# Attention in front of a routed MLP: the u term beside the logits, the state's decay on VectorE, bounds by transposes, another prologue

## The chip, the core and the metric

One core of a Trainium2 chip runs the whole program. The metric is the device time of one execution in microseconds (us), median of three runs. TensorE (PE), VectorE (DVE), ScalarE (ACT), GpSimd (POOL) and the DMA queue of SyncE (SP) each work through their instructions in the order written and wait for each other by semaphores.

## The reference, cut to what matters

```python
for t in range(S):                                   # 4 batches, 8 heads, 768 steps, head size 48
    cur = einsum('bhd,bhe->bhde', u[None] * kt, vt)
    y[:, :, t] = einsum('bhd,bhde->bhe', rt, state + cur)
    state = w[None, :, :, None] * state + einsum('bhd,bhe->bhde', kt, vt)
...
logits = x @ w_gate                                  # x: y by token, 3072 x 384; 8 experts
order = np.argsort(-logits.flatten())                # greedy, 384 tokens to an expert
h = np.maximum(x[mask] @ w1[e], 0.0); out[mask] = h @ w2[e]
...
h = np.maximum(x @ w_in, 0.0); return h * h @ w_out  # a second MLP over all tokens
```

## The kernel before

Attention works in 24 chunks n of 128 tokens, chunk c = n // 4 of batch b = n % 4. Per chunk `prep` (L175, DVE) multiplies r and k by powers of w, `prep_rk` (L179, POOL) makes pr = r*k, `qk` (L209, PE) makes the 128x128 scores of 8 heads in two PSUM banks pA0, pA1, and `am` (L212, DVE) copies their lower triangle over AM, which `diagonal` (L198, POOL) has filled with the u term of each head on its diagonal. That term, cc, is the sum over d of u*r*k: `ruk` (L189, PE) makes it with pr as weights, `ccput` (L193, DVE) copies it out. `state_y` (L221) adds r*T of the state T to pY, `chunk_y` (L228) adds AM*v, and `yev` (L234, ACT) copies pY to YT. `kvm` makes the next state in PSUM: Wd*T (L283), the decay by a diagonal matrix, and kk*v (L287), kk = k*KT from `prep_kk` (L203, POOL); `tput` (L293, ACT) copies it to T. One iteration later YT gives the router's logits (`logits` L242, `lev` L246, `logits_by_token` L249, `lput` L254) and x by token (`by_token` L260, `xput` L269 on ACT, then a DMA to DRAM, xd).

The loop over n writes these out by hand in one order for all engines: at its top what waits for the iteration before (lput, xput, ccput), then work for chunks ahead (prep_rk n+3, diagonal n+2, prep_kk and qk n+1, prep n+4, am n+1), then state_y to tput of chunk n, and at its end by_token n-1, ruk n+3 and logits_by_token n-1. Loads run up to 6 (rk) and 4 (tk) chunks ahead on SP.

Between these, `R.step` issues single DVE instructions of the routing from a list that `pace` fills at n-1 = 8, 16 and 20. `spread` takes the largest and smallest router key of the first 16 chunks over all partitions with `G.partition_all_reduce` (L456, POOL); `grid0` lays 64 thresholds between them (L507 to L510), `count` compares (L520) and counts on PE. After the loop `close0` does the rest; `between` there puts the last chunks' x to DRAM. Then `phase` searches the first expert's threshold in steps of compares (L447, DVE) and counts (L612, PE), the tokens are gathered from xd (L717), and the two MLPs follow, expert by expert, bound by PE.

Of the kernel before, what the change touches and what calls it, by code (L numbers as in the profile page):

```python
# [25 lines left out]
FT = mybir.dt.float32  # L26
# [10 lines left out]
NC = S // C  # L37
# [16 lines left out]
def attention(ctx, tc, a, R, L, xd):  # L54
# [12 lines left out]
    AHEAD_RK, AHEAD_TK = 6, 4  # L67

# [17 lines left out]
    Uw = att.tile([112, 4, 8], FT, name="Uw")  # L86
# [4 lines left out]
    wg = att.tile([128, 2, 2, 64], FT, name="wg")  # L91
# [9 lines left out]
    YT = [att.tile([128, 2, 2, 128], FT, name=f"yt{j}") for j in range(2)]  # L101
    KT = att.tile([128, 400], FT, name="KT")
    V.memset(Pw[:, :, :, 0:1], 1.0)
# [38 lines left out]
    for eng, W, x in ((V, WR, 0), (G, WK, 1)):  # L142
        eng.tensor_tensor(W.rearrange("p i (a b) -> p i a b", a=16),
                          Qw[:112, x, :, :, None].to_broadcast([112, 4, 16, 8]),
                          Pw[:112, x, :, None, :].to_broadcast([112, 4, 16, 8]), op=OP.mult)
    W128 = att.tile([112, 4, 1], FT, name="W128")
    TT = att.tile([112, 4, 128], FT, name="TT")
    Wd = att.tile([112, 2, 4, 64], FT, name="Wd")

    def decays():  # L150
        V.tensor_tensor(Uw, Uw, sq[:112, 0, :, 0:1].to_broadcast([112, 4, 8]), op=OP.mult)
        V.tensor_tensor(W128, sq[:112, 0, :, 6:7], sq[:112, 0, :, 6:7], op=OP.mult)
        G.tensor_tensor(TT, WK, W128.to_broadcast([112, 4, 128]), op=OP.mult)
# [9 lines left out]
    def decay_diagonals():  # L163
        sh = [112, 4, 64]
        for s in range(2):
            G.tensor_tensor(Wd[:, s], ident[:112, None, half(s, 64)].to_broadcast(sh), W128.to_broadcast(sh), op=OP.mult)


    pr, cc, kks, pA, AM, pYs, pk, pts, pls, lts, pms = ({} for _ in range(11))
# [11 lines left out]
    def pm(n):  # L181
        if n not in pms:
            pms[n] = ps.tile([128, 136], FT, name="pm")
        return pms[n]

    def ruk(n, m):

        for i in range(4):
            PE.matmul(pm(m)[:, 128:], pr[n][:, i], Uw[:, i], start=not i, stop=i == 3)  # L189

    def ccput(n, m):
        cc[n] = wk.tile([128, 8], FT, name="cc")
        V.tensor_copy(cc[n], pm(m)[:, 128:])  # L193

    def diagonal(n):

        AM[n] = wk.tile([128, 4, 2, 128], FT, name="AM", bufs=3)
        G.affine_select(AM[n].rearrange("p i s t -> p (i s) t"), cc[n][:, :, None].to_broadcast([128, 8, 128]),  # L198
                        pattern=[[0, 8], [1, 128]], compare_op=OP.is_equal, fill=0.0, base=0, channel_multiplier=-1)
# [31 lines left out]
    def yev(n, s, eng=None):  # L231
        o, x = YT[n % 2][:, s], pYs[n][s]
# [5 lines left out]
    def logits(n):  # L238
# [9 lines left out]
    def logits_by_token(n, m):  # L248
        PE.transpose(pm(m)[:, :128], lts[n], ident)  # L249

    def lput(n, m):
        c, b = divmod(n, B)
        x = pm(m)[:, :128].rearrange("p (s e) -> p e s", s=2)[:, :8]
        V.tensor_reduce(L[:, b * NC + c, :], x, axis=AX.X, op=OP.add)  # L254

    def by_token(n):
        pts[n] = ps.tile([128, 4, 128], FT, name="pt")
        for s in range(2):
            for j in range(2):
                PE.transpose(pts[n][:, 2 * s + j], YT[n % 2][:, s, j], ident)  # L260

# [12 lines left out]
    def kvm(n):  # L274

        c, b = divmod(n, B)
        if c == NC - 1:
            return
        p = pk[n] = ps.tile([128, 4, 64], FT, name="pk")
        if c:  # L280
            for i in range(4):
                for s in range(2):
                    PE.matmul(p[half(s, 64), i], Wd[:, s, i], T[b][:, i], start=not i, stop=False, skip_group_check=True)  # L283
        for i in range(4):
            for s in range(2):
                h = 2 * i + s
                PE.matmul(p[half(s, 64), i], kks[n][:, 48 * h:48 * h + 64], v_of(n, h), start=not c and not i, stop=True,  # L287
                          skip_group_check=True)
# [7 lines left out]
    ok = lambda n: 0 <= n < NCH  # L296
    decays()
    prep(0)
    prep_rk(0)
    decays_by_token()  # L300
    qk(0)
    ruk(0, -3)
    ccput(0, -3)
    diagonal(0)
    prep(1)
    prep_rk(1)
    ruk(1, -2)
    ccput(1, -2)
    prep_kk(0)
    diagonal(1)  # L310
    am(0, 0)
    am(0, 1)
    prep(2)
    prep_rk(2)
    ruk(2, -1)
    decay_diagonals()
# [4 lines left out]
    for n in range(NCH):  # L321
        load_rk(n + AHEAD_RK)
        load_tk(n + AHEAD_TK)
        if n == NCH - B:
            R.cnt0 = ps.tile([128, 512], FT, name="pk")
        if ok(n - 2):
            lput(n - 2, n - 1)
            xput(n - 2)
        if ok(n + 2):
            ccput(n + 2, n - 1)  # L330
        if ok(n + 3):
            prep_rk(n + 3)
        if ok(n + 2):
# [22 lines left out]
        kvm(n)  # L356
        tput(n)
# [6 lines left out]
        if ok(n - 1):  # L364
            logits_by_token(n - 1, n)
        R.step(4)
    n = NCH - 1
    lput(n - 1, n)
    logits(n)
    lev(n)  # L370
    logits_by_token(n, n + 1)
    lput(n, n + 1)
    R.arrive(NC - 1, NC)

    def last():
        xput(n - 1)
        by_token(n)
        xput(n)
# [4 lines left out]
class Routing:  # L383
# [4 lines left out]
    def __init__(self, tc, pool, ident, L):  # L388
        self.tc, self.pool, self.ident, self.L = tc, pool, ident, L
        self.misc = None  # L390
        self.todo, self.wide, self.mms, self.left = [], [], [], 0
        self.fill = lambda n=1: None
        self.lag = 3, 1
# [4 lines left out]
    def make(self):  # L398
# [13 lines left out]
        self.ones = one([128, 128], "onesb", BF)  # L412
        V.memset(self.ones, 1.0)
# [35 lines left out]
    def spread(self, gm):  # L449

        V, G = self.tc.nc.vector, self.tc.nc.gpsimd
        mx = self.tile([128, 2], "mx")
        junk = self.tile([128, NT], "sel")
        return [lambda: V.tensor_reduce(mx[:, 0:1], self.key0, axis=AX.X, op=OP.max),
                lambda: V.tensor_scalar(junk, self.low0, -1.0, -BIG, op0=OP.mult, op1=OP.max, accum_out=mx[:, 1:2]),
                lambda: G.partition_all_reduce(gm, mx, channels=128, reduce_op=bass.bass_isa.ReduceOp.max)]  # L456
# [27 lines left out]
    def arrive(self, c0, c1):  # L484

        V = self.tc.nc.vector
        l, m, cx, oh, lw = (self.chunks(t, c0, c1) for t in (self.L, self.key0, self.cx0, self.oh0, self.low0))
        self.todo.append(lambda: V.tensor_reduce(m, l, axis=AX.X, op=OP.max))
        ops = self.pick(l, m, cx, oh, self.tile([128, B, c1 - c0, E], "eq", FT, 1))
        least = lambda: V.tensor_reduce(lw, l, axis=AX.X, op=OP.min)  # L490
        if c1 < NC:
            self.todo += ops + [least]
        else:

            self.count(c0, c1)
            self.gm1 = self.tile([128, 2], "gm")
            mx0, mx1, red = self.spread(self.gm1)
            self.todo += [ops[0], least, ops[1], mx0, ops[2], mx1, red, ops[3]]

    def grid0(self):  # L500
# [3 lines left out]
        *mx, red = self.spread(gm)  # L504
        pause = lambda: None
        self.todo += mx + [pause, red, pause, pause, pause,
# [584 lines left out]
def _layouts(r, k, v, w, u, w_gate, w1, w2, w_in, w_out):  # L1091
# [13 lines left out]
    ul = np.zeros((112, 4, E), u.dtype)  # L1105
    for h in range(H):
        ul[64 * (h % 2):64 * (h % 2) + D, h // 2, h] = u[h]
    wg = np.zeros((128, 2, 2, 64), w_gate.dtype)
    for h in range(H):
# [8 lines left out]
        "wg": wg.reshape(128, 256),  # L1118
# [25 lines left out]
```

## Time and profile before

| | us |
|---|---|
| median of 3 runs (890.19 to 895.34) | 890.65 |
| profiled execution, device time | 890.34 |
| its span, first to last instruction | 888.3 |
| attention, first instruction to the first gather | 184.26 |

The profiled execution is one of the program's executions; 2.0 us of it lie around the span. In the rows below a time is us from the start of the span, then the length in us, the engine and line of the program, output<-inputs, the shape, and how many instructions the row merges; PEld is the load of TensorE's weights. "[x <-y]" is idle time of that engine just before, and what ended it. An fp32 matmul shows as two records.

### The profile page before, as it was taken

The page shows a single profiled execution, that of the slowest core. Times are in us where ns is not written, and L with a number is a line of the kernel's source. Part 1 is how long each engine was busy: PE and PEld are TensorE (multiplying, and loading weights), DVE is VectorE, ACT ScalarE, POOL GpSimd, SP SyncE. Part 2 cuts the span into 40 slices and gives each one's busy share as a digit, 9 for nine tenths or more (in the row PEclk, how much of TensorE's full clock was granted, in tenths as well). Part 3 has the DMA queues.
Part 4 walks back from the last instruction along what each step waited for, and adds up shares of the span by engine and source line. Part 5 has one row for each costly group of instructions (what it writes and reads, how often), then busy time and mean ns, then how long its engine had stood idle before and what let it go on. Part 6 is the DMA issues. An engine that isn't in the chain of part 4 may idle for free.

```text
span 888.3 us, 16748 instructions
## 1 busy us (share of the span) xinstructions
PE 813.9 (92%) x6497; PEld 775.3 (87%) x6497; DVE 439.5 (49%) x1016; ACT 366.1 (41%) x799; POOL 337.7 (38%) x322
## 2 busy tenths in 40 slices
PE   3899996668788699999999999999999999999997
PEld 2899995548678699999999989999999999999996
DVE  3645443669999735714651573259235512321211
ACT  0233331233354533642464265417533644554443
POOL 5877762138486640504143141405040506204001
PEclk9999997768799899999999999999999999999999
DMA  8775640145535210401231031105010404101000
GB/s 233 214 222 181 189 139 20 38 133 166 173 107 178 62 46 25 129 1 45 60 93 45 1 114 39 45 1 151 2 45 23 130 10 136 52 1 45 1 1 28
DMA packets 37503, 73.78 MB, mean 83 GB/s; under 512 B 5680, under 2 KB 25264, under 8 KB 37424
## 3 DMA queue, kind: packets, MB, share of 16 engines
q1 hardware_dynamic: 34352, 63.28, 23.9%
q0 software_dynamic: 3072, 9.44, 3.3%
q8 instruction: 51, 0.84, 0.4%
q14 instruction: 28, 0.23, 0.1%
HBM read 63.26 MB, written 9.44 MB: 82 GB/s over the span
## 4 chain that ended last, share of the span: by engine, by line
PE 78%; DVE 15%; issue 2%; POOL 1%; DMA 1%; ACT 1%; POOLq 0%; SPq 0%; DVEq 0%; ACTq 0%
PE acc L784 10%; PE acc L785 10%; PE acc L786 10%; PE ph L784 10%; PE ph L786 9%; PE ph L785 9%; PE pA L209 3%; PE pm L189 3%; PE pY L228 2%; PE misc L612 2%; DVE cm L447 2%; DVE raw L835 2%; DVE raw L831 2%; DVE al L962 2%; PE pl L242 2%
## 5 line engine op out<-in xcount | busy, mean ns | idle before, releaser
L781 POOL TENSOR_TENSOR wl<-raw,wh 128x384 fp32r<-128x384 f32 x120 | 125.9, 1067 | 159.6 <-ACT wh L780 131.0
L962 DVE TENSOR_TENSOR al<-t,ah 128x384 fp32r<-128x384 f32 x120 | 86.4, 723 | 158.9 <-ACT t L959 155.6
L784 PE MATMUL ph<-YH,wi 128*128 128x384 f32 x384 | 132.6, 345 | 0.0
L784 PE MATMUL acc<-wo,ah 128*128 128x384 f32 x384 | 131.2, 342 | 0.0
L786 PE MATMUL acc<-wo,al 128*128 128x384 f32 x384 | 130.2, 339 | 0.6 <-POOL al L962 0.6
L785 PE MATMUL acc<-wo,ah 128*128 128x384 f32 x384 | 129.6, 338 | 0.0
L785 PE MATMUL ph<-YL,wi 128*128 128x384 f32 x384 | 129.0, 336 | 0.0
L786 PE MATMUL ph<-YH,wi 128*128 128x384 f32 x384 | 128.9, 336 | 0.0
L977 POOL DMA_INDIRECT out_dram<-rows,idx x24 | 23.7, 989 | 253.3 <-ACT rows L975 249.1
L955 ACT ACTIVATE t<-ph 128x384 f32<-128x384 f32 x128 | 62.5, 488 | 138.0 <-PE ph L786 136.9
L780 ACT ACTIVATE wh<-raw 128x384 fp32r<-128x384 f32 x128 | 65.1, 523 | 65.4 <-PE ph L785 20.8
L925 DVE SCALAR_TENSOR_TENSOR al<-ph,ah 128x384 fp32r<-128x384 f32 x64 | 35.2, 551 | 85.0 <-ACT ah L924 79.2
L786 PEld LDWEIGHTS acc<-wo,al 128*128 128x128 f32 x384 | 73.0, 190 | 1.2 <-POOL al L962 1.2
L785 PEld LDWEIGHTS acc<-wo,ah 128*128 128x128 f32 x384 | 73.0, 190 | 0.0
L784 PEld LDWEIGHTS acc<-wo,ah 128*128 128x128 f32 x384 | 72.9, 190 | 0.1
L784 PEld LDWEIGHTS ph<-YH,wi 128*128 128x128 f32 x384 | 72.6, 189 | 0.3
L785 PEld LDWEIGHTS ph<-YL,wi 128*128 128x128 f32 x384 | 72.7, 189 | 0.0
L786 PEld LDWEIGHTS ph<-YH,wi 128*128 128x128 f32 x384 | 72.5, 189 | 0.0
L785 PE MATMUL acc<-al,wh 128*128 128x384 f32 x192 | 66.1, 344 | 4.0 <-DVE al L925 4.0
L784 PE MATMUL acc<-ah,wh 128*128 128x384 f32 x192 | 68.2, 355 | 1.5 <-ACT ah L924 1.5
L447 DVE TENSOR_TENSOR cm<-key,thr 128x512 bf16<-128x512 f32 (+2 forms) x81 | 68.4, 879 | 0.3
L959 ACT ACTIVATE t<-t 128x384 f32<-128x384 f32 x128 | 67.1, 524 | 2.8
(205 smaller groups left out, 1576.6 us busy)
## 6 DMA issues: line engine op xcount, KB each, us to landing
raw<-in_w_dram SPq DMA_DIRECT2D x128, 192.0 KB, 2.5
rk<-in_rk_dram SPq DMA_DIRECT2D x24, 448.0 KB, 4.5
tk<-in_tk_dram SPq DMA_DIRECT2D x24, 392.0 KB, 8.6
raw<-in_wi_dram SPq DMA_DIRECT2D x16, 384.0 KB, 5.5
raw<-in_wo_dram SPq DMA_DIRECT2D x16, 384.0 KB, 3.0
xd<-xs SPq DMA_DIRECT2D x24, 192.0 KB, 1.8
rows<-xd,idx POOLq DMA_INDIRECT x24
out_dram<-rows,idx POOLq DMA_INDIRECT x24
```

The lines of the kernel that those rows point to most:

```text
L189: PE.matmul(pm(m)[:, 128:], pr[n][:, i], Uw[:, i], start=not i, stop=i == 3)
L209: PE.matmul(pA[n][s][:, i], RK[n][half(s), 1, i], RK[n][half(s), 0, i], start=True, stop=True)
L447: eng.tensor_tensor(cm, key[:, :, None].to_broadcast(sh), th, op=OP.is_ge)
L780: A_.activation(hi, t, AF.Copy)
L781: (eng or G).tensor_tensor(lo, t, hi.bitcast(FT), op=OP.subtract)
L784: PE.matmul(o, l[0], r[0], start=first, stop=False)
L785: PE.matmul(o, l[0], r[1], start=False, stop=False)
L786: PE.matmul(o, l[1], r[0], start=False, stop=last)
L925: later(1, lambda: V.scalar_tensor_tensor(hl, o, 0.0, hh.bitcast(FT), op0=OP.max, op1=OP.subtract))
L955: A_.activation(t, o, AF.Relu)
L959: A_.activation(t, t, AF.Square)
L962: later(2, lambda: (G if p == 0 and f < 8 else V).tensor_tensor(gl, t, gh.bitcast(FT), op=OP.subtract))
```

## The change

(`LATE` is 6; `R.spare` gives the bank of `by_token`.)

- u term: `ruk` and its weights pr leave the loop. `logits` now writes four quarters of 32 partitions of its bank: two with the logits' weights, 32 columns wide, and two with Uw (32 columns wide) as weights and pr[n+3] moving. `lev` and `logits_by_token` carry both; `ccput(n + 2)` reads the u term from the bank that `lput(n - 2)` reads. The first four chunks still use `ruk`.
- diagonals: POOL fills half of AM, ACT the other half by four scaled copies of the identity.
- decay: the diagonal matrices Wd and their 8 matmuls leave `kvm`. `fade` makes tT = T*W128 on DVE, `tput` adds it to kk*v on DVE.
- bounds: `partition_all_reduce` becomes two PE transposes of the broadcast column and a DVE maximum over them.
- the last six chunks' by_token and xput move into `between`.
- prologue: 20 and 6 matmuls whose result nobody reads (`unread`), WK on DVE, Uw and W128 on POOL, TT on ACT, and another order.

```diff
-    YT = [att.tile([128, 2, 2, 128], FT, name=f"yt{j}") for j in range(2)]
+    YT = [att.tile([128, 2, 2, 128], FT, name=f"yt{j}") for j in range(LATE)]
+    trash = ps.tile([128, 512], FT, name="pt")
+    def unread(n):
+        for _ in range(n):
+            PE.matmul(trash, R.ones, R.warm, start=True, stop=True)
+    unread(20)
...
     def decays():
+        G.tensor_tensor(Uw, Uw, sq[:112, 0, :, 0:1].to_broadcast([112, 4, 32]), op=OP.mult)
+        G.tensor_tensor(W128, sq[:112, 0, :, 6:7], sq[:112, 0, :, 6:7], op=OP.mult)
+        for i in range(4):
+            A_.activation(TT[:, i], WK[:, i], AF.Copy, scale=W128[:, i])
...
     def diagonal(n):
         AM[n] = wk.tile([128, 4, 2, 128], FT, name="AM", bufs=3)
+        G.affine_select(AM[n][:, :2].rearrange("p i s t -> p (i s) t"), cc[n][:, 0, :, None].to_broadcast([128, 4, 128]),
+                        pattern=[[0, 4], [1, 128]], compare_op=OP.is_equal, fill=0.0, base=0, channel_multiplier=-1)
+        for h in range(4):
+            A_.activation(AM[n][:, 2 + h // 2, h % 2], ident, AF.Copy, scale=cc[n][:, 1, h:h + 1])
...
+    def logits(n, m):
         p = pls[n] = ps.tile([128, 128], FT, name="pl")
+        q = lambda k: p[32 * k:32 * k + 32]
         for j in range(2):
             for s in range(2):
-                PE.matmul(p[half(s, 64)], wg[:, s, j], YT[n % 2][:, s, j], start=not j, stop=bool(j))
+                PE.matmul(q(2 * s), wg[:, s, j], YT[n % LATE][:, s, j], start=not j, stop=bool(j), skip_group_check=True)
+                PE.matmul(q(2 * s + 1), Uw[:, 2 * s + j], pr[m][:, 2 * s + j], start=not j, stop=bool(j), skip_group_check=True)
...
-        if c:
-            for i in range(4):
-                for s in range(2):
-                    PE.matmul(p[half(s, 64), i], Wd[:, s, i], T[b][:, i], start=not i, stop=False, skip_group_check=True)
...
+    def fade(n):
+        c, b = divmod(n, B)
+        if 0 < c < NC - 1:
+            tTs[n] = wk.tile([112, 4, 64], FT, name="tT")
+            V.tensor_tensor(tTs[n], T[b], W128.to_broadcast([112, 4, 64]), op=OP.mult)
     def tput(n):
         c, b = divmod(n, B)
-        if c < NC - 1:
+        if c == 0:
             A_.activation(T[b], pk[n][:112], AF.Copy)
+        elif c < NC - 1:
+            V.tensor_tensor(T[b], tTs[n], pk[n][:112], op=OP.add)
...
     decays()
     prep(0)
     prep_rk(0)
+    prep(1)
+    qk(0)
+    unread(6)
+    ruk(0)
+    prep_rk(1)
+    diagonal(0)
     decays_by_token()
     am(0, 0)
     am(0, 1)
+    ruk(1)
+    prep_kk(0)
     prep(2)
+    diagonal(1)
     prep_rk(2)
...
         R.step(wide=False)
+        fade(n)
         if ok(n + 1):
             qk(n + 1)
...
         if ok(n - 1):
-            logits(n - 1)
+            logits(n - 1, min(n + 3, NCH - 1))
             lev(n - 1)
...
         if ok(n - 1):
-            by_token(n - 1)
-        if ok(n + 3):
-            ruk(n + 3, n)
+            if n - 1 < NCH - LATE:
+                by_token(n - 1)
+            logits_by_token(n - 1)
...
     def last():
+        for j in range(NCH - LATE, NCH):
+            by_token(j, ("pt", "pA0", "pA1")[j % 3])
+            xput(j)
...
+        def turn():
+            box.append(self.spare())
+            for j in range(2):
+                self.tc.nc.tensor.transpose(box[0][:, j], mx[:, j:j + 1].to_broadcast([128, 128]), self.ident)
-                lambda: G.partition_all_reduce(gm, mx, channels=128, reduce_op=bass.bass_isa.ReduceOp.max)]
+                lambda: turn(),
+                lambda: V.tensor_reduce(gm, box[0], axis=AX.X, op=OP.max)]
```

## Rows read from the trace of the kernel before

**Rows 1.** Busy time by stretches: PE, PEld, DVE, ACT, POOL, granted clock, DMA share, GB/s
```profile
10.00:20.00 10.00, 6.42 (x36) 5.83 (x36) 1.30 (x2) 0.55 (x2) 5.31 (x4) 1.00 1.04 280
...
140.00:150.00 10.00, 6.47 (x53) 5.70 (x55) 1.58 (x4) 0.06 (x1) 4.64 (x4) 0.51 0.00 1
```
**Rows 2.** The chain that ended last: start, length, what; qk(5) in iteration 4
```profile
46.29 1.09 PE pA L209 x16
```
**Rows 3.** The timeline of one iteration, n = 13, TensorE
```profile
97.29 1.16 PE L209 MATMUL pA<-rk 48*128 48x128 f32 x16
...
98.38 0.67 PE L221 MATMUL pY<-rk,T 48*64 48x128 f32 x16
...
98.98 0.42 PEld L242 LDWEIGHTS pl<-yt,wg 128*64 128x64 f32 x8 [0.17 <-issue]
...
99.47 1.09 PE L228 MATMUL pY<-AM,tk 128*64 128x128 f32 x16
...
100.34 0.69 PE L283 MATMUL pk<-T,Wd 112*64 112x64 f32 x16
...
100.81 0.69 PE L287 MATMUL pk<-tk,kk 128*64 128x64 f32 x16
...
101.92 0.96 PE L189 MATMUL pm<-Uw,pr 112*128 112x8 f32 x8
...
102.73 0.31 PE L249 MATMUL pm<-ident,lts 128*128 128x128 f32 x1
...
102.97 1.16 PE L209 MATMUL pA<-rk 48*128 48x128 f32 x16
```
**Rows 4.** The same iteration, VectorE and GpSimd
```profile
97.56 1.22 DVE L175 TENSOR_TENSOR rk<-rk,WRK 112x1024 f32<-112x1024 f32 x1
97.78 1.95 POOL L198 TENSOR_SCALAR_AFFINE_SELECT AM<-cc 128x1024 f32<-128x1024 f32 x1 [1.46 <-DVE cc L193]
...
98.70 1.34 DVE L212 COPY_PREDICATED AM<-mask,pA 128x512 f32<-128x512 int32 x2
...
99.70 1.05 POOL L203 TENSOR_TENSOR kk<-tk,KT 128x400 f32<-128x400 f32 x1
...
100.72 1.27 POOL L179 TENSOR_TENSOR pr<-rk 112x512 f32<-112x512 f32 x1
```
**Rows 5.** The timeline around the all-reduce, iterations 19 and 20
```profile
134.68 0.37 POOL L456 PARTITION_ALL_REDUCE gm<-mx  x1 [5.55 <-issue]
...
142.22 1.25 POOL L179 TENSOR_TENSOR pr<-rk 112x512 f32<-112x512 f32 x1 [7.17 <-issue]
...
143.53 1.88 PE L189 MATMUL pm<-Uw,pr 112*128 112x8 f32 x8 [7.39 <-POOL pr L179]
...
145.64 2.08 PE L209 MATMUL pA<-rk 48*128 48x128 f32 x16
```
**Rows 6.** The timeline of the prologue: the first prep
```profile
7.74 1.22 DVE L175 TENSOR_TENSOR rk<-rk,WRK 112x1024 f32<-112x1024 f32 x1
```
**Rows 7.** Groups by line and shape in attention: total, mean ns | idle before
```profile
L236 DVE COPY yt<-pY 128x256 f32<-128x256 f32 x1 | 0.4, 426 | 2.1 <-PE pY L228 2.1
```
**Rows 8.** VectorE and GpSimd at once: timelines at 27 and at 254 us
```profile
27.04 3.45 DVE L175 TENSOR_TENSOR rk<-rk,WRK 112x1024 f32<-112x1024 f32 x1
27.31 1.09 POOL L198 TENSOR_SCALAR_AFFINE_SELECT AM<-cc 128x1024 f32<-128x1024 f32 x1
...
254.08 1.44 DVE L447 TENSOR_TENSOR cm<-key,thr 128x512 bf16<-128x512 f32 x1
...
254.92 1.47 POOL L816 TENSOR_TENSOR wi<-raw,wi 128x384 fp32r<-128x384 f32 x1
```
**Rows 9.** The timeline behind the loop: the last by_token, the first count
```profile
167.52 1.11 PE L260 MATMUL pt<-ident,yt 128*128 128x128 f32 x4
...
169.53 1.69 PE L612 MATMUL misc<-oh,cm 128*64 128x8 bf16 x24 [0.90 <-DVE cm L447]
```
**Rows 10.** DMA issues of the page: line, count, KB each, us to landing
```profile
xd<-xs SPq DMA_DIRECT2D x24, 192.0 KB, 1.8
```

More of the change, by code (lines that the diff above doesn't have):

```diff
@@ L67, in attention @@
     AHEAD_RK, AHEAD_TK = 6, 4
+    LATE = 6
     RK, TK = {}, {}
@@ L85, in attention @@
     load_rk(0)
-    Uw = att.tile([112, 4, 8], FT, name="Uw")
+    Uw = att.tile([112, 4, 32], FT, name="Uw")
     nc.sync.dma_start(Uw, a["u"])
@@ L90, in attention @@
     load_rk(2)
-    wg = att.tile([128, 2, 2, 64], FT, name="wg")
+    wg = att.tile([128, 2, 2, 32], FT, name="wg")
     nc.sync.dma_start(flat(wg), a["wg"])
@@ L161, in decays_by_token @@
             A_.activation(kt[:, :, s, :], pt[:, :, half(s)], AF.Copy)
-    def decay_diagonals():
-        sh = [112, 4, 64]
-        for s in range(2):
-            G.tensor_tensor(Wd[:, s], ident[:112, None, half(s, 64)].to_broadcast(sh), W128.to_broadcast(sh), op=OP.mult)
-    pr, cc, kks, pA, AM, pYs, pk, pts, pls, lts, pms = ({} for _ in range(11))
+    pr, cc, kks, pA, AM, pYs, pk, pts, pls, lts, pms, tTs = ({} for _ in range(12))
     def v_of(n, h):
@@ L179, in prep_rk, with ruk, ccput @@
         G.tensor_tensor(pr[n], RK[n][:, 0], RK[n][:, 1], op=OP.mult)
[L181 to L186, printed above, removed]
-        for i in range(4):
[L189 to L193, printed above, removed]
+    def ruk(n):
+        p = ps.tile([128, 2, 4], FT, name="pm")
+        for i in range(4):
+            PE.matmul(p[:, i // 2], pr[n][:, i], Uw[:, i, :4], start=not i, stop=i == 3, skip_group_check=True)
+        ccput(n, p)
+    def ccput(n, p):
+        cc[n] = wk.tile([128, 2, 4], FT, name="cc")
+        V.tensor_copy(cc[n], p)
     def diagonal(n):
         AM[n] = wk.tile([128, 4, 2, 128], FT, name="AM", bufs=3)
-        G.affine_select(AM[n].rearrange("p i s t -> p (i s) t"), cc[n][:, :, None].to_broadcast([128, 8, 128]),
-                        pattern=[[0, 8], [1, 128]], compare_op=OP.is_equal, fill=0.0, base=0, channel_multiplier=-1)
+        G.affine_select(AM[n][:, :2].rearrange("p i s t -> p (i s) t"), cc[n][:, 0, :, None].to_broadcast([128, 4, 128]),
+                        pattern=[[0, 4], [1, 128]], compare_op=OP.is_equal, fill=0.0, base=0, channel_multiplier=-1)
+        for h in range(4):
+            A_.activation(AM[n][:, 2 + h // 2, h % 2], ident, AF.Copy, scale=cc[n][:, 1, h:h + 1])
     def prep_kk(n):
@@ L246, in lev, with logits_by_token, lput, by_token @@
         A_.activation(lts[n], pls[n], AF.Copy)
-    def logits_by_token(n, m):
-        PE.transpose(pm(m)[:, :128], lts[n], ident)
-    def lput(n, m):
+    def logits_by_token(n):
+        pms[n] = ps.tile([128, 128], FT, name="pm")
+        PE.transpose(pms[n], lts[n], ident)
+    def lput(n):
         c, b = divmod(n, B)
-        x = pm(m)[:, :128].rearrange("p (s e) -> p e s", s=2)[:, :8]
+        x = pms[n].rearrange("p (s e) -> p e s", s=2)[:, :8]
         V.tensor_reduce(L[:, b * NC + c, :], x, axis=AX.X, op=OP.add)
-    def by_token(n):
-        pts[n] = ps.tile([128, 4, 128], FT, name="pt")
+    def by_token(n, name="pt"):
+        pts[n] = ps.tile([128, 4, 128], FT, name=name)
         for s in range(2):
             for j in range(2):
-                PE.transpose(pts[n][:, 2 * s + j], YT[n % 2][:, s, j], ident)
+                PE.transpose(pts[n][:, 2 * s + j], YT[n % LATE][:, s, j], ident)
     def xput(n, eng=None):
@@ L286, in kvm @@
                 h = 2 * i + s
-                PE.matmul(p[half(s, 64), i], kks[n][:, 48 * h:48 * h + 64], v_of(n, h), start=not c and not i, stop=True,
+                PE.matmul(p[half(s, 64), i], kks[n][:, 48 * h:48 * h + 64], v_of(n, h), start=not i, stop=True,
                           skip_group_check=True)
+    def fade(n):
[3 more added lines that the diff above has]
+            V.tensor_tensor(tTs[n], T[b], W128.to_broadcast([112, 4, 64]), op=OP.mult)
     def tput(n):
         c, b = divmod(n, B)
-        if c < NC - 1:
+        if c == 0:
             A_.activation(T[b], pk[n][:112], AF.Copy)
+        elif c < NC - 1:
+            V.tensor_tensor(T[b], tTs[n], pk[n][:112], op=OP.add)
     ok = lambda n: 0 <= n < NCH
+    R.spare = lambda: ps.tile([128, 2, 128], FT, name="pt")
     decays()
@@ L326, in attention @@
         if ok(n - 2):
[L327 to L330, printed above, removed]
+            lput(n - 2)
+            if n - 2 < NCH - LATE:
+                xput(n - 2)
+            if ok(n + 2):
+                ccput(n + 2, pms[n - 2].rearrange("p (s e) -> p s e", s=2)[:, :, 32:36])
+        elif n == 1:
+            ruk(3)
         if ok(n + 3):
             prep_rk(n + 3)
-        if ok(n + 2):
+        if ok(n + 2) and n:
             diagonal(n + 2)
@@ L356, in attention @@
         kvm(n)
+        if n == 0:
+            ruk(2)
+            diagonal(2)
         tput(n)
@@ L390, in __init__ @@
         self.misc = None
+        self.ones, self.warm = pool.tile([128, 128], BF, name="onesb", bufs=1), pool.tile([128, 512], BF, name="warmb", bufs=1)
         self.todo, self.wide, self.mms, self.left = [], [], [], 0
```

64 lines of the change are left out of this document (20 added, 44 removed).

## The prediction

> **What bounds the kernel now.** I read the busy shares by stretches first. In the loop of attention PE is busy all of every 10 us, while DVE, ACT and POOL are not. Two stretches differ: the prologue, where the DMA queues are full at 280 GB/s and PE works little, and 140 to 150, where PE idles and its granted clock is 0.51 [rows 1]. The chain of waits then says where the loop stands: qk(5) starts at 46.29 [rows 2]. Then the timeline of one iteration: from one qk to the next 5.68 us, with PE parts back to back [rows 3], so a PE instruction that leaves is worth its length, until DVE and POOL [rows 4] become the limit. Last the timeline around the all-reduce: POOL spends 5.55 us before it and 7.17 behind it in "issue", pr comes late, and PE sits idle 7.39 us; its qk then takes 2.08 instead of 1.16, at half clock, 1.2 GHz [rows 5]. Behind attention the change touches nothing, so what it saves moves the rest forward as it is.
>
> **The loop, chunks 4 to 19.** From start to start in the iteration: qk 1.09, state_y 0.60, logits 0.49, chunk_y 0.87, Wd 0.47, kk and by_token together 1.11, ruk 0.81, logits_by_token 0.24; sum 5.68 [rows 3]. Wd and ruk leave: 5.68 - 0.47 - 0.81 = 4.40. Logits go from 8 records to 16. The trace shows no 32-column quarters. If quarters run beside each other as the halves seem to, the u half costs nothing more, 0.49; 16 records of 128 columns in two halves take chunk_y's 0.87; state_y's 16 records in four corners of the array take 0.60 and are nearest. Before the loads of logits PEld waits 0.17 [rows 3], where the array goes from one cut to another, and chunk_y behind now needs one such change more. I take 0.60 + 0.17: a period of 4.68, with bounds 4.40 and 0.87 + 0.17 = 1.04, so 4.95. From qk(5) to qk(20) are 15 periods: 15 x 1.00 = **15.0 us** (11 to 19).
>
> On the tiling there is a rule that speaks against the change: the Trainium skill (TensorEngine Tiling, Key Properties) says that changing the tiling mode, not just the tile, drains TensorE. By that rule the change pays one drain more per iteration; the row's 0.17 agrees in kind, and without it the period is 4.51 and the loop gives 2.5 us more.
>
> **What else must fit into 4.68.** DVE loses nothing and gains fade and the sum in tput. Each handles 112x256; the nearest row is 0.43 for 128x256 [rows 7], bounds 0.2 and 0.7. DVE then has prep 1.22, am 1.34 [rows 4], two of 0.43 and some 0.3 of small copies: 3.7. POOL loses half of the diagonals. That row's 1.95 has waiting in it: it starts inside prep, and without it takes 1.09 [rows 4, 8]; half is 0.55, with kk 1.05 and pr 1.27 [rows 4] 2.87. ACT loses tput and gains four copies of 128 columns, at most 0.43 each as above, 1.7, behind the copy of x; behind them in its queue stands lev, which waits for logits some 2.3 us into the iteration anyway. None reaches 4.68 alone. But prep, fade and POOL's instructions exclude each other: 1.22 + 0.43 + 2.87 = 4.52. That fits with 0.16 to spare if nothing waits in a bad order. tput waits for kvm as before; behind it on DVE stand only the next top's copies, which wait for PE's last transpose, later still. ccput now needs lev and the transpose, both an iteration early; pr(n+3) is needed 2 us earlier than by ruk, but POOL ends it before the iteration's qk is over. DMA: rk, 112x1024, and tk, 128x784 numbers of 4 bytes, are 0.86 MB in, xd 0.2 out [rows 10]; 1.06 MB per period is 225 GB/s against 280 seen [rows 1]: hidden.
>
> At n = 17 to 19 DVE has eight small routing steps of about 0.2 each, then the maximum over the transposes, the thresholds and two compares: 5 to 5.5 us in two of these iterations, and PE waits once for the column to be transposed and for by_token's bank. I charge **2.0** (0.5 to 4).
>
> **The all-reduce.** Before, PE would have gone on at 143.53 - 7.39 = 136.14 with ruk and the transpose, 1.05 together, to qk(21) at 137.19; it came at 145.64 [rows 3, 5]. The transposes replace it, so **8.45 us** come back; if the stall only shrank to a late maximum, some 6.
>
> **The last four chunks.** From qk(21) at 145.64 to 167.52 [rows 5, 9] lie 21.9 us. Iterations without kvm and ruk were worth 3.78 by the prices above and are worth 3.57 now without by_token and with the larger logits, four of them 0.8 less. About 5 us of before ran at half clock [rows 1] and lost about half, 2.5; by_token in iteration 19 is worth 0.5. Together **3.8 us** (2.5 to 5).
>
> **The prologue.** The first prep starts at 7.74 [rows 6] and waits for the weights' powers, as before. WK on DVE and the small products on POOL put its end at about 9.4. From there to qk(5) the instructions that exclude each other are seven preps, seven pr, six half diagonals and five kk: 8.5 + 8.9 + 3.3 + 5.3 = 26.0, so 35.4 at the earliest order, and I add 1.4 for cc(0), which waits for qk(0), the six unread matmuls and ruk: qk(5) at 36.8 instead of 46.29 [rows 2], **9.5 us**. Bounds: 33.8, if the last diagonal and kk fall behind qk(5), and 41, if PE's gaps of 1.5 to 2 us in iterations 0 and 1 bring its clock down. The twenty unread matmuls are hidden behind the wait for prep(0); at half clock, where 128 columns take 0.13 [rows 5], they would last 20 x 0.52 = 10.4, to 11.8, and hold up qk(0) by 2.5. The loads are no limit: rk4 is the tenth transfer, 3.6 MB, 13 us at 280 GB/s.
>
> **What comes behind the loop.** between now holds 24 transposes and six copies to xs, of which two buffers exist. PE stands in line: the first count, at 169.53, is behind them [rows 9]. A group of four takes 1.11 at half clock [rows 9]; six end 6.2 us after the first begins, and the copies, each waiting 1.8 for the transfer two before it [rows 10], make it no shorter. The count comes at 167.52 + 6.2 = 173.7 instead of 169.53, 4.2 later; at full clock the buffers limit and it is 2. The maximum instead of the all-reduce costs DVE about 0.2. I take **-3.9** (-2 to -5). The transfers end before the gather 15 us later.
>
> **Sum.** 15.0 - 2.0 + 8.45 + 3.8 + 9.5 - 3.9 = 30.9. The profiled execution took 890.34, 0.3 below the median of the runs: 890.3 - 30.9 = 859.4, **859 us**.
>
> **Rivals.**
> *The port.* A prep that was ready at 27.04 took 3.45: it let a diagonal of 1.09 pass, and the kk behind it [rows 8]. Now fade stands between cc and prep, the diagonal arrives during fade, and if POOL keeps the port through kk, prep waits 0.55 + 1.05. DVE's period is then 3.7 + 1.6 = 5.3, and the loop gives 15 x 0.38 = 5.7 instead of 15.0: 869. Against it: at 254 a compare and POOL's products took turns, 1.44 and 1.47 each with one wait [rows 8]; then prep waits 0.55 only. On this the Trainium skill (SBUF — State Buffer, Who interferes with whom) says that whoever issues first holds the shared pair for the whole instruction, and that a DVE instruction with two SBUF inputs contends with GpSimd's reads. By that rule the diagonal goes first and prep second, as at 254 and not as at 27.04; the trace shows both.
> *All covers hold.* Quarters cost nothing, 4.51 is the port's period, the prologue reaches 33.8 and the clock behind the loop stays up: 859 - 2.5 - 3 - 2 - 3 = 848.
> *Slower than before.* If the gaps that the new waits leave bring PE to 1.2 GHz inside the loop, qk takes 2.08, and the iteration of 4.68 about 8. Each period at that level loses 3.3; after ten of them the 30.9 are gone, and with all fifteen the time is 859 + 50 = 909. For it: PE was at 0.51 from 140 on. Against it: that came after more than 4 us without a matmul [rows 1, 5], and the loop has no such gap.
> *The stall stays,* because the transposes wait for their bank or the column as long: 859 + 8 = 867.
>
> **How the numbers follow.** The forecast, 853 to 864 with its bounds, 0.52; the port 0.24 (864 to 872); all covers 0.12; the stall 0.07; half clock 0.03; the rest elsewhere. A range from 846 to 871 leaves about 2 in 10 out. Within 1% (8.9 us, about what a measurement here can tell from no change) is reached only if the port and the stall fail together with the prologue, 0.02; slower by over 1% only by the clock, 0.03; faster 0.95.
>
> **What would show it.** Period of qk in the loop 4.6 to 4.8 and PE busy throughout (right), or 5.2 to 5.4 with PE waiting for am and prep lasting 2.8 (the port). No POOL "issue" of 5 us near n = 18. qk(5) near 37. The first count of the search some 6 us behind the first late transposes, at clock 0.5. What would make me wrong most: quarters that don't overlap at all, or a clock that falls in iterations 0 to 3.

## The result, and the profile after

The changed kernel takes **857.05 us** (median of 4 runs, 855.24 to 857.88) against 890.42 for the kernel before, measured beside it: ratio 0.9612, 95% interval 0.9572 to 0.9651. The forecast was 859. The profiled execution took 857.88 us, with a span of 855.9 (before: 888.3). The sum came out 2 us off, but its terms were off by up to 3.6, in both directions.

First the busy time by stretches of the changed kernel (columns as in [rows 1]):

```profile
13.00:15.00 2.00, 1.15 (x9) 0.87 (x10) 1.53 (x4) 1.21 (x6) 0.83 (x2) 1.00 1.01 269
...
16.70:20.00 3.30, 2.58 (x29) 2.39 (x25) 1.72 (x2) 0.66 (x2) 3.30 (x3) 0.50 1.04 260
20.00:25.00 5.00, 3.19 (x17) 3.11 (x19) 2.98 (x6) 1.60 (x6) 4.23 (x5) 0.50 1.03 250
...
60.00:70.00 10.00, 10.00 (x194) 8.48 (x190) 8.87 (x20) 5.90 (x18) 9.08 (x7) 1.00 0.90 249
```

The loop is still bound by PE (10.00 of 10 us), now with DVE and POOL close to it. In the prologue, [rows 1] has a granted clock of 1.00 between 10 and 20 us; here it is 0.50, 1.2 GHz, from about 16.7 on. PE had been busy 1.15 of the 2 us from 13 to 15, and is so for 2.58 of 3.30 while the clock is down. The chain that ended last shows what this costs (start, length, what):

```profile
7.06 12.42 DMA rk<-in_rk_dram
...
21.28 1.32 DVE AM L216 x2
...
22.79 1.84 PE pm L190 x8
24.62 2.01 PE pA L213 x16
...
38.86 1.09 PE pA L213 x16
```

A u term and a qk (L213) run at half clock, where the same qk takes 1.09 later. The last line is qk(5), which answers to [rows 2]. Now TensorE's timeline of iteration 13, as in [rows 3]; of the sixteen matmuls of the logits the first two are shown:

```profile
74.77 1.16 PE L213 MATMUL pA<-rk 48*128 48x128 f32 x16
75.86 0.67 PE L225 MATMUL pY<-rk,T 48*64 48x128 f32 x16
76.46 0.30 PE L249 MATMUL pl<-yt,wg 128*32 128x128 f32 x1
76.47 0.30 PE L250 MATMUL pl<-pr,Uw 112*32 112x128 f32 x1
...
77.04 1.14 PE L232 MATMUL pY<-AM,tk 128*64 128x128 f32 x16
77.96 0.68 PE L292 MATMUL pk<-tk,kk 128*64 128x64 f32 x16
78.58 0.66 PE L269 MATMUL pt<-ident,yt 128*128 128x128 f32 x4
79.07 0.27 PE L258 MATMUL pm<-ident,lts 128*128 128x128 f32 x1
79.27 0.38 PE L213 MATMUL pA<-rk 48*128 48x128 f32 x2
```

The period is 4.50 (5.68 before). The logits, now with the u term, start at 76.46, and chunk_y follows at 77.04: 0.58, where the gating half alone took 0.49 [rows 3]. Gating and u matmuls start 0.01 apart and run beside each other. VectorE and GpSimd in the same iteration, as in [rows 4]:

```profile
75.05 0.42 DVE L299 TENSOR_TENSOR tT<-T,W 112x256 f32<-112x256 f32 x1
75.38 1.65 DVE L180 TENSOR_TENSOR rk<-rk,WRK 112x1024 f32<-112x1024 f32 x1
...
75.29 0.67 POOL L200 TENSOR_SCALAR_AFFINE_SELECT AM<-cc 128x512 f32<-128x512 f32 x1 [0.48 <-DMA rk<-in_rk_dram]
75.93 2.02 POOL L207 TENSOR_TENSOR kk<-tk,KT 128x400 f32<-128x400 f32 x1
```

Prep lets the half diagonal finish (1.65 against 1.22 alone), then runs, and kk waits for it (2.02 against 1.05): they take turns by whole instructions. Around the former all-reduce, and behind the loop, the rows that answer to [rows 5] and [rows 9]:

```profile
102.44 0.40 PE L474 MATMUL pt<-ident,mx 128*128 128x128 f32 x2 [0.61 <-DVE sel L477]
102.77 1.16 PE L213 MATMUL pA<-rk 48*128 48x128 f32 x16
...
107.27 1.16 PE L213 MATMUL pA<-rk 48*128 48x128 f32 x16
...
111.33 1.16 PE L213 MATMUL pA<-rk 48*128 48x128 f32 x16
...
129.87 1.12 PE L269 MATMUL pt<-ident,yt 128*128 128x128 f32 x4
...
132.49 1.06 PE L269 MATMUL pt<-ident,yt 128*128 128x128 f32 x4
...
135.80 0.49 ACT L278 ACTIVATE xs<-pA 128x384 f32<-128x384 f32 x1 [3.43 <-DMA xd<-xs]
136.34 1.12 PE L269 MATMUL pA<-ident,yt 128*128 128x128 f32 x4 [1.94 <-ACT xs L278]
139.34 1.39 PE L633 MATMUL misc<-oh,cm 128*64 128x8 bf16 x24 [1.89 <-ACT xs L278]
```

No 14 us gap is left: qk(20) at 107.27, qk(21) at 111.33. The transposes of the maxima make PE wait 0.61 once, in iteration 18, whose period is 5.51. Behind the loop the third late copy to xs waits 3.43 for a transfer, and the first count comes 9.47 after the first late transpose.

From the starts of qk and of the first count, against those of before (the missing ones, all from the timelines: qk(5) and qk(20) of before at 46.22 and 131.35, qk(5) of after at 38.79; the chain has qk(5) 0.07 later in both kernels):

| stretch | before | after | gain | forecast |
|---|---|---|---|---|
| to qk(5) | 46.22 | 38.79 | 7.4 | 9.5 |
| qk(5) to qk(20) | 85.13 | 68.48 | 16.6 | 13.0 |
| qk(20) to qk(21) | 14.29 | 4.06 | 10.2 | 8.45 |
| to the late transposes | 21.88 | 18.54 | 3.3 | 3.8 |
| to the first count | 2.01 | 9.47 | -7.5 | -3.9 |
| to the end of the span | 718.8 | 716.6 | 2.2 | 0 |

The 2.2 of the last line lies in work that the change doesn't touch. From the first gather to the end it takes 703.9 to 704.6 in before and the two runs below that are made from it, and 700.7 to 703.4 in the changed kernel (702.1) and those made from that. What makes the two groups differ, and the scatter within the second, stays open.

### The profile page after: what moved, and what is told of

The parts are those of the page before. It is cut to its first block, busy times and chain, and to the rows that moved or that the text cites. A ratio compares the mean times of both kernels' runs of the same rounds, so it can differ in the third digit from the quotient of the medians.

```text
span 855.9 us, 16484 instructions
## 1 busy us (share of the span) xinstructions
PE 797.0 (93%) x6303; PEld 747.9 (87%) x6303; DVE 455.6 (53%) x1050; ACT 390.2 (46%) x883; POOL 325.5 (38%) x318
## 4 chain that ended last, share of the span: by engine, by line
PE 78%; DVE 12%; DMA 4%; issue 2%; POOL 2%; ACT 0%; SPq 0%; POOLq 0%; ACTq 0%; DVEq 0%
PE acc L805 11%; PE acc L806 10%; PE acc L807 10%; PE ph L805 10%; PE ph L807 10%; PE ph L806 9%; PE pA L213 3%; PE pY L232 3%; PE misc L633 3%; DMA rk<-in_rk_dram 2%; DVE cm L462 2%; DVE raw L856 2%; PE pl L249 2%; PE pY L225 1%; PE ph L938 1%
## 5 line engine op out<-in xcount | busy, mean ns | idle before, releaser
L983 DVE TENSOR_TENSOR al<-t,ah 128x384 fp32r<-128x384 f32 x120 | 80.8, 677 | 159.2 <-ACT t L980 159.1
L979 ACT ACTIVATE ah<-t 128x384 fp32r<-128x384 f32 x128 | 67.0, 524 | 2.5
```

The costliest lines, as they stand in the source:

```text
L979: A_.activation(gh, t, AF.Square)
L983: later(2, lambda: (G if p == 0 and f < 8 else V).tensor_tensor(gl, t, gh.bitcast(FT), op=OP.subtract))
```

## The experiments

Times are medians; the ratio is to the kernel before, run on the same chip in turn.

**Bounds alone.** The kernel before with the transposes in place of the all-reduce; the routing steps around it stand in another order, without the pauses between them.

```diff
-                lambda: G.partition_all_reduce(gm, mx, channels=128, ...)]
+                lambda: turn(),
+                lambda: V.tensor_reduce(gm, box[0], axis=AX.X, op=OP.max)]
```

> The kernel before with one part of the change: the two all-reduces become transposes and a maximum. Theory (the all-reduce costs the idle time before and behind it and a spell at half clock): no POOL issue of 5 us, from qk(20) to qk(21) about 6.5 instead of 14.3 us, and some 2.5 us more from iterations that no longer run at 1.2 GHz; the time falls by 9 to 11, to about 880. Rival (the stall shrinks to a wait for a late maximum, because the transposes wait for by_token's bank and for DVE): it falls by 6 at most, to 884 or above, and PE shows an idle time of over 2 us before the transposes.

Measured: 879.57 us, ratio 0.9867 (0.9828 to 0.9906). TensorE's timeline of this run:

```profile
125.17 0.38 PE L460 MATMUL pt<-ident,mx 128*128 128x128 f32 x2
...
131.16 1.16 PE L209 MATMUL pA<-rk 48*128 48x128 f32 x16
136.84 1.16 PE L209 MATMUL pA<-rk 48*128 48x128 f32 x16
```

The transposes wait for nothing, and qk(20) to qk(21) is one ordinary period, 5.68 instead of 14.3. The rival, a stall that only shrinks to a late maximum, is out.

**The decay alone.** The kernel before with fade and the sum on VectorE, without the eight Wd matmuls.

```diff
-                    PE.matmul(p[half(s, 64), i], Wd[:, s, i], T[b][:, i], start=not i, stop=False, ...)
...
+            V.tensor_tensor(tTs[n], T[b], W128.to_broadcast([112, 4, 64]), op=OP.mult)
...
+            V.tensor_tensor(T[b], tTs[n], pk[n][:112], op=OP.add)
```

> The kernel before with one part of the change: the decay matmuls leave, fade and the sum in tput go to DVE; the diagonals stay whole on POOL and the u term stays at the end of the iteration. Theory (PE sets the period, and what leaves PE is worth its length): period of qk 5.68 - 0.47 = 5.2 in iterations 4 to 19, the time falls by 7 to 8, to 883. Rival (prep, fade and POOL exclude each other, 1.22 + 0.42 + 1.09 + 1.05 + 1.27 = 5.05, and fade lets the diagonal in ahead of prep): POOL is late for pr, the period stays above 5.4 and the time falls by 4 at most.

Measured: 885.92 us, ratio 0.9957 (0.9936 to 0.9978). The period is 5.21, which is the 0.47 of the Wd row [rows 3], and qk(20) starts 6.8 us earlier. But qk(20) to qk(21) grows from 14.3 to 15.3: part of what the loop gains is waited away at the all-reduce, and the median falls by 4.6 only (before, in these runs: 890.5).

**The u term undone.** The changed kernel with the u term as four matmuls of its own again, and the gating logits in halves.

```diff
-                PE.matmul(q(2 * s + 1), Uw[:, 2 * s + j], pr[m][:, 2 * s + j], ...)
...
+            if ok(n + 3):
+                pms[n - 1] = ps.tile([128, 136], FT, name="pm")
+                ruk_late(n + 3, pms[n - 1])
             logits_by_token(n - 1)
```

> The changed kernel with the u term of chunk n+3 back as four matmuls of its own at the end of the iteration, into spare columns of the tile of the logits' transposes, and the gating logits alone in halves of 64 columns, as in the kernel before. Theory: the four quarters of the changed kernel's logits run abreast (0.57 us for sixteen records, 0.49 for the eight before), so that what the change took off is the whole of the separate step: the period goes from 4.50 to 5.2, and over sixteen periods the time to 868 (866 to 870). Rival: part of the 0.7 us was gained elsewhere (order of the queue, the wait for the copied diagonal values), and the period is 4.7 to 4.9, as the forecast for the changed kernel had it, with the time at 860 to 863.

Measured: 868.62 us, ratio 0.9734 (0.9697 to 0.977), periods of 5.20 to 5.21. TensorE's timeline of one iteration:

```profile
66.32 0.95 PE L195 MATMUL pm<-Uw,pr 112*128 112x4 f32 x8
67.13 0.31 PE L261 MATMUL pm<-ident,lts 128*128 128x128 f32 x1
...
69.05 0.66 PE L252 MATMUL pl<-yt,wg 128*64 128x128 f32 x8
```

The separate step holds PE 0.81 from start to start, and the logits go back to 0.49. So the summing in quarters is worth 0.7 per period and 11.6 us in all (2.5 of them ahead of qk(5), which starts at 41.33 here), about as much as the bounds with 10.9; its eight added records cost about 0.1.

**Diagonals whole on GpSimd.** The changed kernel with one affine_select for all eight heads, as before.

```diff
-        for h in range(4):
-            A_.activation(AM[n][:, 2 + h // 2, h % 2], ident, AF.Copy, scale=cc[n][:, 1, h:h + 1])
```

> The changed kernel with one part undone: the diagonals are whole on POOL again, no scaled copies on ACT. The period was 4.50 in the changed kernel, with PE busy throughout. Theory (the instructions that exclude each other come next after PE: 4.5 with the half diagonal, 5.05 with the whole): period 5.0 to 5.2, and 8 to 10 us slower than the changed kernel, about 866; PE shows gaps. Rival (PE sets the period with room beside it): period stays 4.5 to 4.6, time 856 to 858.

Measured: 860.09 us, ratio 0.9658 (0.9624 to 0.9691). GpSimd's timeline of this run, with VectorE's fade in the first line:

```profile
77.08 0.57 DVE L298 TENSOR_TENSOR tT<-T,W 112x256 f32<-112x256 f32 x1
77.33 1.27 POOL L200 TENSOR_SCALAR_AFFINE_SELECT AM<-cc 128x1024 f32<-128x1024 f32 x1
78.58 2.01 POOL L206 TENSOR_TENSOR kk<-tk,KT 128x400 f32<-128x400 f32 x1
80.55 1.28 POOL L184 TENSOR_TENSOR pr<-rk 112x512 f32<-112x512 f32 x1
81.80 1.26 POOL L200 TENSOR_SCALAR_AFFINE_SELECT AM<-cc 128x1024 f32<-128x1024 f32 x1
```

GpSimd has no gap left here and goes round in 4.47, just what PE needs; eleven of the fifteen periods stay at 4.50, three are 5.1 and that of iteration 18 is 5.96 instead of 5.51. Both statements were wrong: halving the diagonals is worth some 3 us by the medians, not 9, and the periods show that it is not nothing. My sum of instructions that exclude each other, 5.05, took whole lengths. In the rows the start of one lies under the end of another: fade starts at 77.08, while pr of the round before runs to 77.37, and lasts 0.57 instead of 0.42; the diagonal behind it starts at 77.33 and lasts 1.27 instead of 1.09 [rows 8]. They still hold each other up, but a round takes 4.47.

**Late transposes in the loop.** The changed kernel with the by-token transposes of all chunks but the last in the loop again.

```diff
-            if n - 1 < NCH - LATE:
+            if n - 1 < NCH - 1:
                 by_token(n - 1)
```

> The changed kernel with one part undone: by_token and xput of all chunks but the last stand in the loop again. Behind the loop the changed kernel needs 9.5 us from the first late transpose to the first count, before it was 2.0. Theory (the late transposes stand in front of the search in PE's line, at half clock and waiting for the buffers of xs; in the loop they cost 0.5 each): the loop's end comes 2 to 2.5 us later, the first count 7.5 sooner, together 5 us faster than the changed kernel, about 852. Rival (the search waits for something else behind the loop, DVE or the DMA of xd): the first count moves by less than 3, and the time stays within 1 us of 857.

Measured: **851.57 us**, ratio 0.9557 (0.9523 to 0.959). The last qk starts 1.5 us later (120.42 instead of 118.95), but the first count is at 133.43 instead of 139.34 (2 to 2.5 later and 7.5 sooner were expected). In this kernel holding six chunks back loses 5.9 us to the first count: little PE work is saved in the loop, and PE's queue is blocked behind it.

**Six buffers of xs.** The changed kernel with one more word.

```diff
-        xs = wk.tile([128, 4, 2, 48], FT, name="xs")
+        xs = wk.tile([128, 4, 2, 48], FT, name="xs", bufs=6)
```

> The changed kernel with six buffers instead of two for the by-token copies behind the loop (xs). In the changed kernel the first late transpose is at 129.87 us and the first count of the routing at 139.34; the third late copy on ScalarE waits 3.4 us for the transfer of an earlier one, which lands 4.15 us after its issue. Theory (buffers): without that wait the stretch of late transposes is bound by their instructions at half clock, 6 to 6.5 us in all, so that the first count starts at 136 to 136.8 and the time is 854. Rival (clock): at 0.50 the transposes and copies alone take the 9.5 us, the first count stays within 0.7 us of 139.3, and the time at 857.

Measured: 852.16 us, ratio 0.9561 (0.9532 to 0.959). The fourth group of late transposes, ScalarE's third late copy and the first count:

```profile
132.44 0.66 PE L269 MATMUL pt<-ident,yt 128*128 128x128 f32 x4
132.69 0.49 ACT L278 ACTIVATE xs<-pA 128x384 f32<-128x384 f32 x1 [0.36 <-PE pA L269]
...
134.56 0.90 PE L633 MATMUL misc<-oh,cm 128*64 128x8 bf16 x24 [0.58 <-ACT xs L278]
```

The copy waits 0.36 for PE instead of 3.43 for a transfer; from the first of the six groups to the count it is 4.73 instead of 9.47, even less than expected. Part of that is the clock: it is 0.50 in both kernels up to 132, here 0.72 from 132 to 133 and 1.00 from 133 to 138, in the changed kernel 0.50 up to 138. Up to the fourth group, 0.66 long here and 1.06 there, the rows of PE are the same in both, so it isn't shown that the buffers brought the clock back. The two together are 4.7 of the 7.5 us lost behind the loop; with the 6 to 6.5 expected at half clock the wait alone would be some 3, an estimate.

**Unread matmuls in the prologue.** The changed kernel with sixteen more.

```diff
     ruk(1)
+    spin = ps.tile([128, 512], FT, name="pl")
+    unread(4, spin)
...
+            unread(6, spin)
             ruk(2)
             diagonal(2)
+            unread(6, spin)
```

> The changed kernel with sixteen unread 128x512 bf16 matmuls more in the prologue, where TensorE waits for loads and diagonals: four behind the second chunk's u term, six ahead of and six behind the third's. In the changed kernel the granted clock is 0.50 from 15 to 30 us, and qk(5) starts at 38.8 where 36.8 was forecast. Theory A (clock): the gaps at 13 to 15 us let it fall; filled, the stretch from 15 to 30 us shows a granted clock of 0.9 or more, the u terms of chunks 2 and 3 take about 1.0 instead of 1.8 to 2.1 us, qk(3) starts 2 to 3 us earlier, qk(5) at 36 to 37, and the time is 855 to 856. Rival B (loads): the DMA engines are busy all the time from 5 to 30 us, so that whatever the clock is, qk(5) starts at 38 to 39 and the time stays at 857, or is up to 1 us longer for the added work.

Measured: 852.22 us, ratio 0.9561 (0.9533 to 0.9589); qk(3) at 29.13 (30.99), qk(5) at 36.93 (38.79). Busy time by stretches of this run:

```profile
16.70:20.00 3.30, 3.00 (x37) 2.12 (x34) 3.30 (x2) 0.66 (x2) 3.30 (x3) 1.00 1.06 277
20.00:25.00 5.00, 3.68 (x31) 2.72 (x31) 3.79 (x6) 2.37 (x9) 4.54 (x5) 0.92 1.02 258
25.00:30.00 5.00, 5.00 (x71) 4.12 (x71) 4.27 (x6) 2.45 (x9) 2.78 (x4) 0.74 0.84 220
```

The clock stays up until 25 us; from 25 to 30 it is 0.74, less than the 0.9 expected. qk(5) comes 1.9 us earlier, with the DMA engines as full as ever up to 25 (1.06 and 1.02): the clock was part of the limit. Of the 4.8 us in the median only these 1.9 belong to the prologue. In this execution the third late copy waits 1.15 for its transfer instead of 3.43, which gives 2.0 more up to the count; the rest lies behind it.

**Load order.** The changed kernel with rk3 and rk4 ahead of the values of chunks 1 and 2.

```diff
-    load_tk(1)
     load_rk(3)
+    load_rk(4)
+    load_tk(1)
     load_tk(2)
```

> The changed kernel with another order of loads in the prologue: the r and k of chunks 3 and 4 before the values of chunks 1 and 2, instead of behind them. In the changed kernel the preparation of chunk 4 waits until 19.5 us for a load that takes from 7.1 to 19.5 in the chain of waits. Theory B (loads): the preparation of chunk 4 starts at about 18, and qk(2) and qk(3) 1 to 1.5 us earlier; qk(5) then starts at 37.3 to 38 and the time is 855.5 to 856.5. Rival A (clock): at half clock TensorE's own queue is the limit from 16 to 30 us, the load moves nothing, qk(5) stays within 0.4 us of 38.8, and the time at 857. A third way: the values of chunk 1 now come late, and TensorE waits for them; then qk(3) starts later than 31.0.

Measured: 858.52 us, ratio 0.963 (0.9602 to 0.9659); qk(5) at 38.53, 0.3 earlier; the median is 1.5 above that of the changed kernel, not below it. VectorE's timeline:

```profile
14.63 6.58 DVE L181 TENSOR_TENSOR rk<-rk,WRK 112x1024 f32<-112x1024 f32 x3
21.14 1.32 DVE L217 COPY_PREDICATED AM<-mask,pA 128x512 f32<-128x512 int32 x2
```

No wait for a load is left before the masked copies of chunk 1, and they start at 21.14 instead of 21.28. Three preps last 6.58 instead of the 3 x 1.22 that the first prep's row gives [rows 6], since they take turns with GpSimd. So the load of 12.42 us that the chain of waits names covers another limit of the same length.

**One instruction moved.** The changed kernel with chunk 4's prep behind these copies in iteration 0.

```diff
-        if ok(n + 4):
+        if ok(n + 4) and n:
             prep(n + 4)
...
             am(n + 1, 1)
+        if n == 0:
+            prep(4)
```

> The changed kernel with one instruction moved: in iteration 0, VectorE prepares chunk 4 behind the masked copies of chunk 1's scores instead of ahead of them. In the changed kernel, and with the loads reordered too, these copies start at 21.1 to 21.3 us, behind preparations that take turns with GpSimd; the copy of chunk 2's u values is queued behind them, chunk 3's u term waits for its PSUM tile, and qk(2) for that. Theory (VectorE's queue): the copies start at about 18.0, qk(2) moves from 24.55 to 21.3 to 22.0, and qk(5) by 1.5 to 3 us; the time is 854 to 855.5. If TensorE's gap is also shorter, its granted clock may come back sooner, and qk(5) moves by up to 4 us. Rival (loads): the values of chunk 1 and the preparation of chunk 4 then come last, and qk(5) stays within 0.7 us of 38.8 (time 857).

Measured: 856.29 us, ratio 0.9609 (0.9583 to 0.9636). VectorE's timeline, and one stretch of busy time:

```profile
17.71 1.32 DVE L216 COPY_PREDICATED AM<-mask,pA 128x512 f32<-128x512 int32 x2
18.93 2.30 DVE L180 TENSOR_TENSOR rk<-rk,WRK 112x1024 f32<-112x1024 f32 x1
21.14 0.15 DVE L195 COPY cc<-pm 128x8 f32<-128x8 f32 x1
```

```profile
20.00:25.00 5.00, 3.58 (x25) 3.56 (x24) 2.98 (x4) 2.82 (x9) 5.00 (x6) 0.52 1.02 282
```

The copies start 3.6 us earlier, but qk(2) gains only 1.3 (23.21): prep(4) slipped in front of the copy of chunk 2's u values, and the clock still fell. In the profiled execution qk(5) is at 36.63, 2.2 earlier, its mean granted clock 0.962; four of the six runs have 0.953 to 0.956, and the median gains 0.8 only.

**Combinations.** Two kernels of three edits each, all shown above: late transposes in the loop, unread matmuls, and first the load order, then in its place the moved prep (the last two lines are that exchange).

```diff
-            if n - 1 < NCH - LATE:
+            if n - 1 < NCH - 1:
...
+    unread(4, spin)
...
-    load_rk(4)
+            prep(4)
```

> The changed kernel with three edits at once: all but the last chunk's by-token transposes in the loop (851.57 us by itself), the sixteen unread matmuls in the prologue, and the chunk loads before the values. If clock and loads both bind in the prologue, the two gains add to qk(5) at 35.5 to 36.5, and the time is 848.5 to 849.5. If the loads alone bind, it is about 850; if the clock alone binds, about 849.5; if neither, it stays at 851.5. In each case the periods behind iteration 18 are those of the kernel with the transposes in the loop (4.8, 4.2, 4.5, 4.0).

> The changed kernel with three edits: by-token transposes of all but the last chunk in the loop, sixteen unread matmuls more in the prologue, and the preparation of chunk 4 behind the masked copies of chunk 1. If the queue of VectorE and the clock are separate limits, qk(5) starts at 34 to 35.5, and the time is 846.5 to 848. If they cover each other, it is that of the run with three edits before it, 849, with qk(5) at 36.5 to 37.

Measured: 849.03 us (ratio 0.9532, 0.9503 to 0.9562), with qk(5) at 36.89; and **848.39 us** (0.9526, 0.9499 to 0.9554), with qk(5) at 35.68 and the clock at 1.00 throughout the prologue. The first gains nothing from the load order; in the second the moved prep and the clock add in part (3.1, where they bring 2.2 and 1.9 alone). The medians, 0.6 apart, don't tell the two from each other; both are below the changed kernel's. Next in line there are a load again (0.52 of waiting for rk ahead of a prep at 23.23) and GpSimd's queue.

## Why the prediction came out near

**The loop: right in mechanism, one wait counted twice.** The period was forecast at 4.68, bounds 4.40 and 4.95, and is 4.50. The step at fault is the price of the logits' quarters, 0.60 + 0.17: they take 0.58. state_y's 0.60 runs from its start to that of the logits, so it already holds the wait of 0.17 ahead of the logits' loads [rows 3]; I added that wait again. Without it the sum gives 4.51. The wait itself came as forecast. PEld's first load of the logits and its loads of chunk_y in iteration 13, and below them those of chunk_y before:

```profile
76.46 0.11 PEld L249 LDWEIGHTS pl<-yt,wg 128*32 128x32 f32 x1 [0.17 <-issue]
...
77.03 0.90 PEld L232 LDWEIGHTS pY<-AM,tk 128*64 128x64 f32 x16 [0.20 <-issue]
```

```profile
99.36 0.96 PEld L228 LDWEIGHTS pY<-AM,tk 128*64 128x64 f32 x16
```

Behind the quarters chunk_y's loads wait 0.20; behind the halves, before and with the u term undone, they wait for nothing. So the 0.09 by which the logits grew is less than this one wait: these rows show no time of its own for the u half beside the gating half. The Trainium skill (TensorEngine Tiling (Array Packing), Key Properties) says that a change of tiling mode drains TensorE. The trace agrees, with 0.17 and 0.20 at the two changes. The charge of 2.0 for the routing steps was 1.0: one iteration of 5.51.

**The all-reduce: right, with an omission.** The 8.45 us were the wait for pr. The remaining 1.8 of the 10.2 lie in iteration 19 itself, which lost ruk, Wd and by_token like the others; I had priced only 0.5 of it, among the last chunks. Bounds alone, measured by itself, gave 10.9 of the time.

**The last four chunks: near.** From qk(21) to the last qk 3.7 came back (11.30 to 7.62), and 0.3 of it went again between there and the late transposes (10.58 to 10.92).

**The port: refuted.** The rival at 869 had POOL keep the port through kk. Prep waits for the half diagonal only, 0.43, and kk then waits for prep, as at 254 us in [rows 8]. The Trainium skill (SBUF — State Buffer, Who interferes with whom) calls the port pair that the two engines share an exclusive lock, and says that the order of issue decides who blocks. The rows of iteration 13 agree, with the diagonal first at 75.29 and prep behind it at 75.38. The sum of 4.52 that I set against the period took whole lengths, though their starts overlap: fade runs to 75.47 under the diagonal's start, and the diagonal takes 0.67 instead of 0.63 without fade (at 22.71). The cover is thin, though: with whole diagonals on POOL it is gone at times, for 3 us.

**The prologue: 2 us short, and the reason given for the bound applied.** I forecast qk(5) at 36.8 and 41 if PE's gaps bring its clock down; they did, to half, and it came at 38.8. Keeping the clock up until 25 us brings 36.9, and the moved prep 36.6. No run takes the other parts of the new prologue back, so how its 7.4 us divide among them stays open. "The loads are no limit" was not what the chain of waits showed afterwards, but the reordered loads gave back 0.3 us: rk4 landed at 19.5, not at the 13 us of the forecast, and the statement held for a reason that I had not named, the order of the instructions on VectorE and GpSimd.

**Behind the loop: wrong by half.** The term -3.9 was -7.5. It failed in the sentence that the copies, "each waiting 1.8 for the transfer two before it", make the stretch "no shorter" than PE's 6.2: a least time was used as the time. With two buffers and transfers that land undelayed, the stretch from the first late transpose to the first count is 7.5 (with the unread matmuls, and with the u term undone). In the changed kernel the third copy waits for a transfer that took 4.15, not 1.8, and the stretch is 9.47. The view of DMA issues and that of one stretch show the cause to look at:

```profile
xd<-xs SPq DMA_DIRECT2D x24, 192.0 KB, 3.2
```

```profile
q8 instruction: 1, 0.02, 1.0%
```

The first is the page's median of all 24 (1.8 in [rows 10]); the second is the stretch from 129 to 139 us of the changed kernel (queue and kind: packets, MB, share of 16 engines). Of its six transfers four land in 1.9, and the first two in 4.15 and 3.76. A load of instructions (q8) starts in the same stretch, between 132 and 133. Six kernels here have six late transposes and two buffers. In four of them such a load starts while the first two transfers are under way, and the third copy waits 3.43 (the changed kernel), 3.36 (diagonals whole), 3.11 (load order) and 3.25 (moved prep). In the other two none does: with the unread matmuls it starts at 128.3, ahead of the first copy, with the u term undone none starts from 143 to 152, and the third copy waits 1.15 and 1.14. All six fit a load of instructions that delays the transfers, but no run moves that load alone, so this is argued, not shown.

These errors, +3.6 and +1.8 against -2.1, -0.5 and -3.6, nearly cancel, which is luck; the 2.2 of untouched work did the rest. With the three losses alone, 6.2, the time would have been 865.6, outside the forecast's own bounds of 853 to 864, though inside the wide range of 846 to 871.

## What to carry to other kernels

An instruction that leaves a full TensorE is worth its start-to-start time, and in this loop small matmuls on other quarters of the array came nearly free. A start-to-start time already holds the wait ahead of the next instruction: don't charge it twice. Work put off to behind a loop is dear where an in-order queue has to pass it: count the buffers that it goes through, and price their waits with the longest transfer of the trace, not the median. A wait named by the chain may hide another of the same length: move the load and look before believing it.

## What the hardware showed that I had not expected

TensorE's granted clock fell to 1.2 GHz in the prologue, around gaps that I had taken for harmless. In the changed kernel PE is busy 1.15 of the 2 us from 13 to 15 and all of the next 1.7, and then the clock is 0.50 until 30 us, the last 5 us of which PE is busy throughout. With the one instruction moved the same stretch from 13 to 15 is again 1.15 busy, yet the clock holds at 1.00 until 20 and falls only then, to 0.52. With the late transposes in the loop, whose prologue is the same, PE is busy 1.27 of those 2 us, and the clock falls there already (0.67). So the moment isn't set by one gap alone. With the unread matmuls, 1.88 of those 2 us, it holds until 25 and is 0.74 from 25 to 30. The gaps cost more by the clock than by themselves: a u term of 1.84 instead of 1.03, a qk of 2.01 instead of 1.09.

Two transfers among six alike took 4.15 and 3.76 us to land instead of 1.9, beside a load of instructions, and with two buffers they stopped ScalarE, PE and the routing's first count in turn.

Sixteen matmuls on four quarters of the array take 0.58 from start to start, a wait of 0.20 for the change of cut included, where eight on two halves take 0.49.
